# Transposing P by 64-row pairs, x a group ahead, and q scaled on ScalarE, in a cached-attention kernel

## The chip, the cores and the metric

The kernel runs on one core of one Trainium2 chip. The metric is the device time of one execution in microseconds. Executions of one kernel mostly agree within some 0.3% (an execution over 1.5% above its kernel's fastest would be called slow and left out). Ratios are the mean time of one kernel's fast runs over that of the other's fast runs of the same rounds, so they are not quite the ratio of the medians quoted beside them. "Faster" or "slower" needs 2%.

PSUM is the memory that TensorE writes its results to; it is divided into banks, and emptying a bank is called eviction here. A *row tile* is a group of rows of TensorE's array that works as a smaller array of its own.

Two more words are used throughout. A *step* is one group of four heads of one pair of batches: 128 steps make the run. A *phase* is 32 steps with one set of weights: there are four, and between them comes a *weight switch*.

## The reference, cut to what matters

Two independent attention blocks (A and B), each with 16 batches, 64 queries, 32 heads of 128, and a cache of 512 keys:

```python
q = (x @ wq).reshape(B, Sq, H, Dh).transpose(0, 2, 1, 3)          # x: 16 x 64 x 640
scores = einsum("bhqd,bhkd->bhqk", q, k_cache) * (Dh ** -0.5)     # k_cache: 16 x 32 x 512 x 128, bf16
p = softmax(scores)
o = einsum("bhqk,bhkd->bhqd", p, v_cache)
out = o.transpose(0, 2, 1, 3).reshape(B, Sq, H * Dh) @ wo         # wo: 4096 x 640
```

Nearly all bytes are K and V: each is read once. One step reads two K tiles and two V tiles of 512 KB.

## The kernel before: the parts that matter

A planner gives each operation a place in time, `AT`, in units of a step; the place sets only the order on each engine and the order in which SyncE queues the loads. Waits follow from what each operation reads and writes. Rings give the depth: six steps of K (`NK = 6`), four of V (`NV = 4`).

```python
AT = dict(XT=-0.998, XE=-0.828, XS=1.064, QP=-0.639, QE=-0.339, KT=(-1.008, -0.378), S=0,
          EX=(0.14, 0.192, 0.454, 0.611), RC=(0.31, 0.63), NM=(0.476, 0.739, 0.793, 0.91), TR=(0.854, 1.001),
          TE=(0.983, 1.034), PV=1.464, OE=1.653, OP=2.236, OA=2.301, OV=2.96, ST=3.466, ...)
# QP: Q projection (TensorE)        QE: scale q out of PSUM       KT: K transposed by VectorE
# S: scores (TensorE)               EX: exp (ScalarE)             NM: P times 1/sum (GpSimd)
# TR: transpose P (TensorE)         TE: copy P^T out of PSUM      PV: P @ V (TensorE)
# OE: O out of PSUM (ScalarE)       OP: output projection         XT: transpose x (TensorE)
```

The three operations that the change touches:

```python
def em_TR(e, op):                          # two per step: 8 transposes of 128 x 128 into one PSUM bank
    for t in range(8):
        last = e.transpose(pt_ps[:, t, :], pn_ring[:, op.idx % NPN, t].rearrange("q s k -> q (s k)"), ident[:, :])

def em_QE(e, op):                          # on VectorE
    ins = e.tensor_scalar(qs_ring[:, op.idx % NQ]..., ps[:, 0, :], scale, None, ALU.mult)

def em_PV(e, op):                          # 64 matmuls; s = 0 and 1 are row halves of the array, in two banks
    for a in range(2):
        for b in range(2):
            for t in range(8):
                for s in range(2):
                    rows = slice(64 * s, 64 * s + 64)
                    last = e.matmul(o_ps[:, s, col:col + 64], v_ring[rows, n % NV, b, a, t, :],
                                    pT_ring[rows, (2 * n + a) % NT, t, 64 * b:64 * b + 64],
                                    start=(t == 0), stop=(t == 7), tile_position=(64 * s, 0))
```

## Time and profile before

| what | before |
|---|---|
| time, median of 3 runs | 779.46 us (779.11 to 781.23) |
| span of the profiled run | 777.3 us |
| bytes moved, mean rate | 295.20 MB, 380 GB/s |
| TensorE, VectorE, ScalarE, GpSimd busy | 91%, 78%, 53%, 51% |

From the page of the kernel before: the row of the DMA engines' rate in 40 slices of the span, and the groups of the P transposes (matmuls, then weight loads), of P @ V and of the scaling of q. In a group line the numbers after the first bar are the busy time in us and the mean of one instruction in ns.

```profile
GB/s 318 389 395 397 394 396 395 394 396 391 392 387 399 398 400 400 400 394 394 387 389 395 397 397 397 397 397 398 374 387 388 398 398 399 400 398 400 400 254 15
...
L632 PE MATMUL ps<-ident,pn_ring 128*128 128x128 bf16 x2048 | 159.8, 221 | 2.7 <-DVE pT_ring L638 1.3
L632 PEld LDWEIGHTS ps<-ident,pn_ring 128*128 128x128 bf16 x2048 | 115.7, 98 | 65.8 <-DVE pT_ring L638 51.2
L650 PE MATMUL ps<-pT_ring,v_ring 64*128 64x64 bf16 x8192 | 142.3, 190 | 7.7 <-DMA v_ring<-in_A_v_cache_dram 4.0
...
L573 DVE TENSOR_SCALAR qs_ring<-ps 128x512 bf16<-128x512 f32 x128 | 85.3, 667 | 0.6 <-PE ps L567 0.5
```

I take some 400 GB/s for all that these engines give here; and TensorE is 91% busy at the same time: the kernel has two limits close to one another, and neither figure says which one counts where.

The window table of the same run, for the steady stretch of the fourth phase, and for two stretches around the end of the loads. The columns are: the window, its length, busy us (and instructions) of TensorE's matmuls, its weight loads, VectorE, ScalarE and GpSimd, then the granted clock, the mean share of the DMA engines, and GB/s.

```profile
620.00:736.00 116.00, 114.84 (x2957) 87.32 (x2977) 99.68 (x175) 68.51 (x197) 56.51 (x84) 1.00 1.04 399
746.00:750.00 4.00, 3.08 (x55) 1.82 (x41) 2.49 (x4) 1.85 (x7) 0.23 (x1) 1.00 0.98 348
750.00:754.00 4.00, 3.98 (x123) 2.71 (x121) 4.00 (x8) 1.20 (x4) 2.69 (x4) 1.00 0.20 75
```

In 620-736 us the DMA engines move 399 GB/s and TensorE is busy for 114.84 of 116 us. By 750 us the rate has collapsed: the loads are over but for stragglers, and 27 us of computing remain.

A step's rhythm, from TensorE's timeline (start in us, duration in us, line, operation; the output projection's lines are left out). P @ V is L650, the P transposes L632, scores L590, the Q projection L567.

```profile
703.53 1.28 PE L567 MATMUL ps<-xT_ring,wqp_sb 128*128 128x128 bf16 x20
704.74 1.11 PE L650 MATMUL ps<-pT_ring,v_ring 64*128 64x64 bf16 x64
705.78 0.62 PE L632 MATMUL ps<-ident,pn_ring 128*128 128x128 bf16 x8
706.33 1.13 PE L590 MATMUL ps<-kt_ring,qs_ring 32*64 32x512 bf16 x32
707.40 0.62 PE L632 MATMUL ps<-ident,pn_ring 128*128 128x128 bf16 x8
...
708.94 1.28 PE L567 MATMUL ps<-xT_ring,wqp_sb 128*128 128x128 bf16 x20
710.16 1.02 PE L650 MATMUL ps<-pT_ring,v_ring 64*128 64x64 bf16 x58
```

From one P @ V to the next there are 5.42 us (704.74 to 710.16). Over the run the intervals repeat as 5.41, 5.42, 5.41, 5.69 us; the fourth holds the transposes of x.

### The profile page before, as it was taken

To read this page: it belongs to the slowest core of one execution; us is meant where nothing else is said; L and a number is where in the kernel's file an instruction comes from. 1 tells how busy PE (TensorE), PEld (TensorE's weight loads), DVE (VectorE), ACT (ScalarE), POOL (GpSimd) and SP (SyncE) were. 2 spreads that over 40 slices of the span, in tenths; PEclk is the share of its full clock that TensorE was granted. 3 is DMA by queue.
4 is the path that set the end of the run, shared out by engine and by line. 5 is a ranking of instruction groups with operands and counts; after the bars stand their busy time and mean duration, and the time that the engine had idled before them with its cause. 6 is when DMAs were issued, how large, how long until landed. Compare 5 with 4: busy or idle time off the path is not lost.

```text
span 777.3 us, 40034 instructions
## 1 busy us (share of the span) xinstructions
PE 708.3 (91%) x17953; PEld 534.6 (69%) x18081; DVE 607.9 (78%) x1062; ACT 412.2 (53%) x1185; POOL 394.6 (51%) x566
## 2 busy tenths in 40 slices
PE   4559999999999999999988999999987899999994
PEld 3446777777777777777765777777765677777763
DVE  3537888888888888888766888888866788888873
ACT  2235656555555555555544555556554456565642
POOL 5424455555944454544843455454773454545441
PEclk9979999999999999999998999999999999999999
DMA  8999999999999999999999999999999999999960
GB/s 318 389 395 397 394 396 395 394 396 391 392 387 399 398 400 400 400 394 394 387 389 395 397 397 397 397 397 398 374 387 388 398 398 399 400 398 400 400 254 15
DMA packets 130096, 295.20 MB, mean 380 GB/s; under 512 B 9216, under 2 KB 31744, under 8 KB 130048
## 3 DMA queue, kind: packets, MB, share of 16 engines
q1 hardware_dynamic: 127744, 292.06, 99.4%
q10 hardware_dynamic: 2304, 2.62, 0.9%
q8 instruction: 15, 0.25, 0.1%
q14 instruction: 33, 0.27, 0.1%
HBM read 292.03 MB, written 2.62 MB: 379 GB/s over the span
## 4 chain that ended last, share of the span: by engine, by line
PE 54%; SPq 27%; DMA 14%; issue 2%; DVE 2%; ACT 0%; DVEq 0%; ACTq 0%
SPq L531 13%; PE ps L567 11%; PE ps L590 11%; SPq L524 11%; PE ps L632 11%; PE ps L650 11%; PE ps L666 7%; DMA kn_ring<-in_B_k_cache_dram 6%; DMA v_ring<-in_A_v_cache_dram 5%; PE ps L669 4%; DMA kn_ring<-in_A_k_cache_dram 2%; SPq L517 2%; DMA xn_ring<-in_A_x_dram 1%; DVE kt_ring L580 1%; PE ps L545 1%
## 5 line engine op out<-in xcount | busy, mean ns | idle before, releaser
L625 POOL TENSOR_SCALAR pn_ring<-p_ring,recip 128x512 bf16<-128x512 bf16 x512 | 344.9, 692 | 360.8 <-DVE recip L620 360.5
L605 ACT ACTIVATE p_ring<-ps 128x512 bf16<-128x512 f32 x512 | 298.7, 596 | 163.8 <-PE ps L590 161.2
L580 DVE STREAM_TRANSPOSE kt_ring<-kn_ring 128x1024 f32<-128x1024 f32 x256 | 315.1, 1231 | 41.1 <-DMA kn_ring<-in_B_k_cache_dram 24.6
L638 DVE COPY pT_ring<-ps 128x1024 bf16<-128x1024 bf16 x256 | 172.1, 672 | 56.9 <-PE ps L632 56.4
L657 ACT ACTIVATE oT_ring<-ps 128x512 bf16<-128x512 f32 x128 | 76.4, 597 | 183.3 <-PE ps L650 163.4
L590 PE MATMUL ps<-kt_ring,qs_ring 32*64 32x512 bf16 x4096 | 147.8, 397 | 24.6 <-DVE qs_ring L573 23.7
L567 PE MATMUL ps<-xT_ring,wqp_sb 128*128 128x128 bf16 x2560 | 166.8, 221 | 2.4 <-POOL wqp_sb L539 1.2
L567 PEld LDWEIGHTS ps<-xT_ring,wqp_sb 128*128 128x128 bf16 x2560 | 153.0, 114 | 18.8 <-ACT p_ring L605 2.2
L632 PE MATMUL ps<-ident,pn_ring 128*128 128x128 bf16 x2048 | 159.8, 221 | 2.7 <-DVE pT_ring L638 1.3
L632 PEld LDWEIGHTS ps<-ident,pn_ring 128*128 128x128 bf16 x2048 | 115.7, 98 | 65.8 <-DVE pT_ring L638 51.2
L650 PE MATMUL ps<-pT_ring,v_ring 64*128 64x64 bf16 x8192 | 142.3, 190 | 7.7 <-DMA v_ring<-in_A_v_cache_dram 4.0
L650 PEld LDWEIGHTS ps<-pT_ring,v_ring 64*128 64x128 bf16 x8192 | 126.9, 95 | 20.8 <-DMA v_ring<-in_A_v_cache_dram 5.4
L669 PE MATMUL ps<-wo_sb,oT_ring 128*128 128x128 bf16 x512 | 112.9, 220 | 8.0 <-ACT oT_ring L657 0.9
L666 PE MATMUL ps<-wo_sb,oT_ring 128*128 128x512 bf16 x384 | 119.6, 383 | 0.0
L605 ACT ACTIVATION_READ_ACCUMULATOR p_ring<-ps 128x1 f32 x512 | 105.1, 205 | 0.0
L590 PEld LDWEIGHTS ps<-kt_ring,qs_ring 32*64 32x64 bf16 x4096 | 55.4, 104 | 66.2 <-DVE qs_ring L573 26.6
L573 DVE TENSOR_SCALAR qs_ring<-ps 128x512 bf16<-128x512 f32 x128 | 85.3, 667 | 0.6 <-PE ps L567 0.5
L666 PEld LDWEIGHTS ps<-wo_sb,oT_ring 128*128 128x128 bf16 x512 | 50.5, 99 | 47.1 <-issue 1.7
L679 DVE TENSOR_TENSOR acc<-acc,ps 128x128 f32<-128x128 f32 x96 | 27.5, 287 | 49.0 <-PE ps L669 48.6
L669 PEld LDWEIGHTS ps<-wo_sb,oT_ring 128*128 128x128 bf16 x512 | 50.5, 99 | 0.0
L620 DVE RECIPROCAL recip<-rowsum 128x2 f32<-128x2 f32 x256 | 36.1, 141 | 2.9 <-ACT p_ring L605 2.8
L545 PE MATMUL ps<-ident,xn_ring 128*128 128x128 bf16 x160 | 15.0, 227 | 16.5 <-ACT oT_ring L657 10.4
(25 smaller groups left out, 121.1 us busy)
## 6 DMA issues: line engine op xcount, KB each, us to landing
kn_ring<-in_A_k_cache_dram SPq DMA_DIRECT2D x128, 512.0 KB, 12.4
v_ring<-in_A_v_cache_dram SPq DMA_DIRECT2D x128, 512.0 KB, 11.6
kn_ring<-in_B_k_cache_dram SPq DMA_DIRECT2D x128, 512.0 KB, 12.5
v_ring<-in_B_v_cache_dram SPq DMA_DIRECT2D x128, 512.0 KB, 10.2
ws_ring<-in_A_wq_dram SPq DMA_DIRECT2D x8, 640.0 KB, 12.2
wo_sb<-in_A_wo_dram SPq DMA_DIRECT2D x8, 640.0 KB, 12.3
ws_ring<-in_B_wq_dram SPq DMA_DIRECT2D x8, 640.0 KB, 12.5
wo_sb<-in_B_wo_dram SPq DMA_DIRECT2D x8, 640.0 KB, 12.6
```

What stands on the lines that cost most here:

```text
L524: ins = e.dma_start(kn_ring[:, n % NK, b, :], src)
L531: ins = e.dma_start(v_ring[:, n % NV, b].rearrange("p a t d -> p a (t d)"), src)
L567: last = e.matmul(ps[:, 0, f * 128:(f + 1) * 128], w[:, kt, f, :], xT_ring[:, xs, kt, :], start=(kt == 0), stop=(kt == KT - 1))
L580: ins = e.transpose(dst, kn_ring[:, n % NK, b, :].bitcast(F32))
L590: last = e.matmul(ps[64 * b:64 * b + 64, i, :], qs_ring[rows, n % NQ, f, b, :], kt_ring[rows, n % NKT, b, :, f // 2, :, f % 2], start=(f = ...
L605: ins = e.activation(dst, src, ACTF.Exp, scale=1.0, accum_out=rowsum[:, h:h + 1])
L625: ins = e.tensor_scalar(pn_ring[:, (h // 2) % NPN, :, h % 2, :], p_ring[:, (h // 2) % NP, :, h % 2, :], recip[:, (h // 2) % NR, h % 2:h % ...
L632: last = e.transpose(pt_ps[:, t, :], pn_ring[:, op.idx % NPN, t].rearrange("q s k -> q (s k)"), ident[:, :])
L638: ins = e.tensor_copy(pT_ring[:, op.idx % NT].rearrange("p t q -> p (t q)"), pt_flat)
L650: last = e.matmul(o_ps[:, s, col:col + 64], v_ring[rows, n % NV, b, a, t, :], pT_ring[rows, (2 * n + a) % NT, t, 64 * b:64 * b + 64], star ...
L666: last = e.matmul(out_ps0, oT, wo_sb[:, 4 * j + h4, 0:N0], start=(j == 0 and h4 == 0), stop=(j == NJ - 1 and h4 == 3))
L669: last = e.matmul(out_ps1, oT, wo_sb[:, 4 * j + h4, N0:D], start=(h4 == 0), stop=(h4 == 3))
```

## The change

Its intent: give TensorE and VectorE less to do.

- P is transposed by 16 matmuls of 64 rows instead of 8 of 128, alternating between the row halves of the array, as P @ V does. The Trainium skill (TensorEngine Tiling (Array Packing), Key Properties and Gotcha 1) says that row tiles load weights and multiply in parallel, but must not write one PSUM bank at the same time; hence the two banks. The second one is shared with O, so transposes, their copies, P @ V and the eviction of O now exclude one another (`B5`).
- x is transposed in the bank of the output projection, between two groups, one group ahead, kept in SBUF, and copied by GpSimd.
- q is scaled by ScalarE instead of VectorE.
- All places `AT` were set anew, so the orders of the engines and of the loads differ too.

```diff
-    AT = dict(XT=-0.998, XE=-0.828, XS=1.064, QP=-0.639, QE=-0.339, KT=(-1.008, -0.378), S=0,
-              EX=(0.14, 0.192, 0.454, 0.611), RC=(0.31, 0.63), NM=(0.476, 0.739, 0.793, 0.91), TR=(0.854, 1.001),
-              TE=(0.983, 1.034), PV=1.464, OE=1.653, OP=2.236, OA=2.301, OV=2.96, ST=3.466, WP0=-1.75, WP1=-2.974)
+    AT = dict(XT=-2.594, XE=-2.103, XC=-0.826, QP=-0.625, QE=-0.284, KT=(-1.051, -0.379), S=0,
+              EX=(0.262, 0.298, 0.389, 0.649), RC=(0.547, 0.697), NM=(0.571, 0.642, 0.8, 1.158), TR=(1.059, 1.236),
+              TE=(1.121, 1.538), PV=1.655, OE=1.933, OP=2.167, OA=2.291, OV=2.255, ST=3.374, WP0=-1.75, WP1=-1.488)
 ... (x: load queued earlier, XT into the output bank, XE into xs_sb, XC copies xs_sb to xT_ring; cut)
-        add("dve", "QE", n, n + AT["QE"], [], [("SB", 0), ("qs", n % cfg.NQ)])
+        add("act", "QE", n, n + AT["QE"], [], [("SB", 0), ("qs", n % cfg.NQ)])
 ...
-                [("PTB",)])
-            add("dve", "TE", m, n + AT["TE"][a], [], [("PTB",), ("pT", m % cfg.NT)])
+                [("B5",)])
+            add("dve", "TE", m, n + AT["TE"][a], [], [("B5",), ("pT", m % cfg.NT)])
 ... (PV and OE likewise from OB to B5; waits that move with it; cut)
-        OUT_BANK, O_BANK, PT_BANK = 4, 5, 7
-        pt_flat = ps[:, PT_BANK, :].bitcast(BF16)
-        pt_ps = pt_flat.rearrange("p (t q) -> p t q", t=8)
+        PT_BANK, O_BANK, OUT_BANK = 4, 5, 7
+        pt_flat = ps[:, PT_BANK:PT_BANK + 2, :].bitcast(BF16)[:, :, 0:512]
 ...
-            ins = e.tensor_scalar(qs_ring[:, op.idx % NQ].rearrange("p f b q -> p (f b q)"), ps[:, 0, :], scale, None,
-                                  ALU.mult)
+            ins = e.activation(qs_ring[:, op.idx % NQ].rearrange("p f b q -> p (f b q)"), ps[:, 0, :], ACTF.Copy,
+                               scale=scale)
 ...
             for t in range(8):
-                last = e.transpose(pt_ps[:, t, :], pn_ring[:, op.idx % NPN, t].rearrange("q s k -> q (s k)"),
-                                   ident[:, :])
-                first = first or last
+                for b in range(2):
+                    rows = slice(64 * b, 64 * b + 64)
+                    last = e.transpose(pt_flat[:, b, 64 * t:64 * t + 64],
+                                       pn_ring[rows, op.idx % NPN, t].rearrange("q s k -> q (s k)"),
+                                       ident[rows, rows], tile_position=(64 * b, 0))
+                    first = first or last
```

The new order on TensorE is: P @ V, scores, first P transpose, output projection, second P transpose, Q projection. Before it was: P @ V, first P transpose, scores, second P transpose, output projection, Q projection.

## The prediction

> **What bounds the kernel now.** Two things, one after the other. The page gives 295.2 MB moved, and the slices show the DMA engines full from start to almost the end (window table: share 1.04; 399 GB/s in 620-736 us, 380-390 GB/s where weights are loaded with K and V). The last bytes land near 751 us; the span ends at 777.3 us, so about 26.5 us of computing are left when the loads are over. Between the weight switches TensorE sets the pace: it is 97-99% busy in 60-190, 230-340, 420-540 and 620-736 us, and P@V starts come every 5.41, 5.42, 5.41, 5.69 us (mean 5.48), which the timeline shows to be filled with matmuls. K and V of one step are 2.097 MB, at 399 GB/s 5.25 us. So in the last phase the loads run ahead of the arithmetic until the rings stop them (the queue waits 48.8 us for P@V to free V buffers), and this lead is the long tail. In the first 50 us TensorE also waits some 14 us for the second x tile (wait list: eviction of O <- x load, 14.9 us), but the DMA moves 389-396 GB/s meanwhile.
>
> **What the change does, per step of 128.**
> - TensorE: two transposes of 8 x 128 rows (0.45 us each) become 16 x 64-row ones, alternating between row halves. P@V has that very form: 64 in 0.99 us, so 16 need about 0.25 us: saving 0.4 us. The Trainium skill (TensorEngine Tiling (Array Packing), Key Properties) says that row tiles run in parallel, which P@V agrees with, and that changing the tiling mode drains the array. There are two more mode changes per step; from P transposes before scores (0.55 us against 0.45 us of loads) I estimate 0.1 us each. Net 0.2 to 0.4 us: a step of 5.1 to 5.25 us.
> - VectorE loses the scaling of q (0.67 us), ScalarE gains about 0.6 us. ScalarE is 53% busy, VectorE 78%: good.
> - x goes through a saved copy, 0.7 us on GpSimd once in four steps, off the path. The earlier x load should end the 14 us stall, without saving DMA time.
> - The second transpose bank is now shared with O. Transpose, copy, transpose, copy, P@V, eviction are serial: 0.25+0.7+0.25+0.7+1.1+0.6 us plus handoffs, about 4.3 us, under 5.2 us, with other matmuls between.
>
> **Critical path.** Loads cannot end much earlier: a little is won where the queue waits for buffers (397 against 399 GB/s; 363-387 GB/s in 548-568 us). I expect 746-750 us. With computing at the loads' pace the tail is only the latency after the last loads: from the start of the last P@V to the end took 10.1 us (767.2 to 777.3, 6 us of it the store); the last K needs transpose, scores, exp, normalisation, transposes first, so 12 to 16 us. Span about 761 us; measured time is 2.2 us longer.
>
> **Prediction: 763 us, 2.1% faster, 8 in 10 within 755 to 771.** Faster by over 2%: 0.53; within 2%: 0.45; slower by over 2%: 0.02.
>
> **What would show it.** P-transpose groups of about 0.25 us; P@V intervals of 5.1-5.3 us, DMA-paced, with more idle TensorE and waits for K or V landings; queue waits for P@V much below 48.8 us; DMA still at 395-400 GB/s; time from last landing to end 12-16 us instead of 26.5; no 14 us wait near 35-50 us.
>
> **What would make it wrong.** If the shared bank stalls TensorE or mode changes eat the saving, steps stay at 5.4 us and the time is 770-779 us. If the last K is issued further ahead, or loads gain more from freer buffers, 755 us.

## More of the kernel before

TensorE's program is long, so its middle is a hardware loop of four steps:

```python
lo = next(i for i, o in enumerate(pe) if o.kind == "QP" and o.idx == cfg.FIRST)               # FIRST = 4
hi = next(i for i, o in enumerate(pe) if o.kind == "QP" and o.idx == cfg.FIRST + cfg.PERIOD)  # PERIOD = 4
reps = (N - 1 - cfg.FIRST) // cfg.PERIOD                                                      # 30 turns
...
for op in prog[:lo]:                       # straight code
    emit(e, op, p, {})
with e.Fori(0, reps):                      # the loop: steps 4 to 123
    ...
for op in prog[lo + size * reps:]:         # straight code again: the end of the run
    emit(e, op, p, taken)
```

## The result, and the profile after

The kernel after takes 778.58 us (median of 4 runs, 777.16 to 779.55) against 779.91 us before in the same rounds: ratio 0.998, 95% interval 0.9958 to 1.0002. The time is the same. The forecast of 763 us, and its range of 755 to 771 us, were wrong.

The lines of the page after that answer to those of before:

```profile
GB/s 313 388 395 397 396 393 397 393 396 393 389 388 399 399 398 401 399 394 398 387 387 393 397 397 397 396 398 398 386 378 389 395 398 400 399 400 399 400 258 16
...
L656 PE MATMUL ps<-pT_ring,v_ring 64*128 64x64 bf16 x8192 | 142.7, 191 | 24.2 <-DMA v_ring<-in_B_v_cache_dram 11.1
...
L637 PEld LDWEIGHTS ps<-ident,pn_ring 64*128 64x128 bf16 x4096 | 74.6, 95 | 108.6 <-ACT oT_ring L663 58.9
...
L637 PE MATMUL ps<-ident,pn_ring 64*128 64x64 bf16 x4096 | 105.1, 192 | 17.2 <-DVE pT_ring L644 11.2
...
L576 ACT ACTIVATE qs_ring<-ps 128x512 bf16<-128x512 f32 x128 | 76.4, 597 | 23.4 <-PE ps L570 23.4
```

TensorE's matmuls are busy 34 us less (708.3 to 674.1 us), VectorE 64 us less. Q's scaling takes 597 ns on ScalarE instead of 667 on VectorE. The rates of the DMA engines are nearly those of before, slice by slice. So the work went away, and the time did not.

The windows after, for the same stretches:

```profile
620.00:736.00 116.00, 110.05 (x3362) 81.38 (x3380) 91.64 (x157) 79.20 (x215) 61.97 (x93) 1.00 1.04 399
746.00:750.00 4.00, 2.65 (x29) 1.50 (x30) 0.69 (x1) 1.26 (x4) 0.00 (x0) 0.61 0.96 354
750.00:754.00 4.00, 3.83 (x126) 2.89 (x132) 3.45 (x7) 2.43 (x6) 1.80 (x3) 0.96 0.26 95
```

TensorE has 5 us more idle time in 620-736 us. In 746-750 us it is busy for only 2.65 of 4 us, and its granted clock, which is 1.00 before the change, is down to 0.61 there.

The rhythm of a step after (P @ V is L656, scores L593, transposes L637, Q projection L570):

```profile
702.69 1.11 PE L656 MATMUL ps<-pT_ring,v_ring 64*128 64x64 bf16 x64
703.76 1.14 PE L593 MATMUL ps<-kt_ring,qs_ring 32*64 32x512 bf16 x32
704.83 0.41 PE L637 MATMUL ps<-ident,pn_ring 64*128 64x64 bf16 x16
...
706.36 0.41 PE L637 MATMUL ps<-ident,pn_ring 64*128 64x64 bf16 x16
706.70 1.31 PE L570 MATMUL ps<-xT_ring,wqp_sb 128*128 128x128 bf16 x20
707.95 1.11 PE L656 MATMUL ps<-pT_ring,v_ring 64*128 64x64 bf16 x64
```

Here a step takes 5.26 us (702.69 to 707.95). Over the run the intervals repeat as 5.22, 5.50, 5.25, 5.65 us: a mean of 5.405 against 5.4825 us before. I had forecast 5.1 to 5.25.

And the end of the run. These are TensorE's instructions after idle time for which the trace shows no releaser ("issue": the sequencer had nothing to hand on), from the timeline, first of the kernel before in 740-748 us, then of the kernel after in 739-749 us. The bracket gives the idle us before the instruction.

```profile
741.73 0.23 PE L632 MATMUL ps<-ident,pn_ring 128*128 128x128 bf16 x1 [0.73 <-issue]
...
747.66 0.43 PE L590 MATMUL ps<-kt_ring,qs_ring 32*64 32x512 bf16 x6 [0.86 <-issue]
```

```profile
740.60 0.23 PE L675 MATMUL ps<-wo_sb,oT_ring 128*128 128x128 bf16 x1 [1.87 <-issue]
...
747.01 0.65 PE L593 MATMUL ps<-kt_ring,qs_ring 32*64 32x512 bf16 x7 [2.54 <-issue]
...
748.54 0.31 PE L675 MATMUL ps<-wo_sb,oT_ring 128*128 128x128 bf16 x1 [0.34 <-issue]
```

All of these fall behind the loop, where TensorE has passed into straight code: its timeline puts the Q projection of step 124, the first operation behind the loop, at 736.57 us before and at 733.87 us after. The second stall after has a sequel: in the window 748-750 us the granted clock is 0.50, and from the first P transpose there to the second it takes 2.79 us (747.59 to 750.38), against 1.53 us at full clock. A ledger of the span makes the account. It is worked out from the starts of P @ V in the timelines; steps are counted from 0, step 100 is the first one clear of the last weight switch, step 127 the last.

| | start of P@V 100 | 22 steps, 100 to 122 | five steps, 122 to 127 | from there to the end | span |
|---|---|---|---|---|---|
| before | 617.0 | 120.8 (5.49 a step) | 29.4 | 10.1 | 777.3 |
| after | 615.7 | 119.4 (5.43 a step) | 32.0 | 10.1 | 777.2 |

The change gains 1.3 us up to step 100, 1.4 us in the next 22 steps, and gives 2.6 us back in the five steps behind the loop.

### The profile page after: what moved, and what is told of

The parts are those of the page before. It is cut to its first block, busy times and chain, and to the rows that moved or that the text cites. A ratio compares the mean times of both kernels' runs of the same rounds, so it can differ in the third digit from the quotient of the medians.

```text
span 777.2 us, 44414 instructions
## 1 busy us (share of the span) xinstructions
PE 674.1 (87%) x20001; PEld 492.0 (63%) x20129; DVE 544.4 (70%) x934; ACT 484.3 (62%) x1297; POOL 404.8 (52%) x582
## 4 chain that ended last, share of the span: by engine, by line
PE 41%; SPq 25%; DMA 18%; POOL 5%; issue 5%; DVE 4%; ACT 0%; DVEq 0%; ACTq 0%
SPq L528 12%; SPq L535 11%; PE ps L570 9%; PE ps L656 9%; PE ps L593 8%; DMA v_ring<-in_B_v_cache_dram 7%; PE ps L672 6%; POOL pn_ring L628 5%; PE ps L637 5%; DMA v_ring<-in_A_v_cache_dram 5%; PE ps L675 4%; DMA wo_sb<-in_B_wo_dram 2%; DMA kn_ring<-in_B_k_cache_dram 2%; DMA wo_sb<-in_A_wo_dram 2%; DVE pT_ring L644 2%
## 5 line engine op out<-in xcount | busy, mean ns | idle before, releaser
L583 DVE STREAM_TRANSPOSE kt_ring<-kn_ring 128x1024 f32<-128x1024 f32 x256 | 312.8, 1229 | 79.9 <-DMA kn_ring<-in_B_k_cache_dram 47.7
L644 DVE COPY pT_ring<-ps 128x1024 bf16<-128x1024 bf16 x256 | 176.2, 688 | 78.8 <-PE ps L637 72.6
L570 PE MATMUL ps<-xT_ring,wqp_sb 128*128 128x128 bf16 x2560 | 170.6, 223 | 19.8 <-issue 13.6
L570 PEld LDWEIGHTS ps<-xT_ring,wqp_sb 128*128 128x128 bf16 x2560 | 151.0, 115 | 28.8 <-issue 16.4
L656 PE MATMUL ps<-pT_ring,v_ring 64*128 64x64 bf16 x8192 | 142.7, 191 | 24.2 <-DMA v_ring<-in_B_v_cache_dram 11.1
L593 PE MATMUL ps<-kt_ring,qs_ring 32*64 32x512 bf16 x4096 | 148.0, 398 | 8.5 <-issue 6.1
L656 PEld LDWEIGHTS ps<-pT_ring,v_ring 64*128 64x128 bf16 x8192 | 127.3, 95 | 38.9 <-DMA v_ring<-in_B_v_cache_dram 14.5
L637 PEld LDWEIGHTS ps<-ident,pn_ring 64*128 64x128 bf16 x4096 | 74.6, 95 | 108.6 <-ACT oT_ring L663 58.9
L637 PE MATMUL ps<-ident,pn_ring 64*128 64x64 bf16 x4096 | 105.1, 192 | 17.2 <-DVE pT_ring L644 11.2
L672 PE MATMUL ps<-wo_sb,oT_ring 128*128 128x512 bf16 x384 | 119.4, 382 | 0.0
L608 ACT ACTIVATION_READ_ACCUMULATOR p_ring<-ps 128x1 f32 x512 | 101.7, 199 | 0.0
L576 ACT ACTIVATE qs_ring<-ps 128x512 bf16<-128x512 f32 x128 | 76.4, 597 | 23.4 <-PE ps L570 23.4
L593 PEld LDWEIGHTS ps<-kt_ring,qs_ring 32*64 32x64 bf16 x4096 | 56.0, 104 | 42.7 <-issue 8.0
L685 DVE TENSOR_TENSOR acc<-acc,ps 128x128 f32<-128x128 f32 x96 | 27.4, 285 | 37.4 <-PE ps L675 37.2
L542 POOL COPY wqp_sb<-ws_ring 128x1280 bf16<-128x1280 bf16 x16 | 20.0, 1253 | 15.6 <-DMA ws_ring<-in_A_wq_dram 8.2
```

The costliest lines, as they stand in the source:

```text
L570: last = e.matmul(ps[:, 0, f * 128:(f + 1) * 128], w[:, kt, f, :], xT_ring[:, xs, kt, :], start=(kt == 0), stop=(kt == KT - 1))
L583: ins = e.transpose(dst, kn_ring[:, n % NK, b, :].bitcast(F32))
L593: last = e.matmul(ps[64 * b:64 * b + 64, i, :], qs_ring[rows, n % NQ, f, b, :], kt_ring[rows, n % NKT, b, :, f // 2, :, f % 2], start=(f = ...
L608: ins = e.activation(dst, src, ACTF.Exp, scale=1.0, accum_out=rowsum[:, h:h + 1])
L637: last = e.transpose(pt_flat[:, b, 64 * t:64 * t + 64], pn_ring[rows, op.idx % NPN, t].rearrange("q s k -> q (s k)"), ident[rows, rows], t ...
L644: ins = e.tensor_copy(pT_ring[:, op.idx % NT].rearrange("p b t q -> p b (t q)"), pt_flat)
```

## The experiments

The theories put to the test, as they arose:

- **A**: up to the last weight switch TensorE waits for loads in any case, so only what comes behind it counts: the pace of some 22 steps, and the stalls that TensorE suffers as it leaves its loop for straight code while the DMA engines are full.
- **B** (rival): the loads alone set the time, with a fixed latency behind them, whatever TensorE does.
- **C**: without the stalls, the end is the landing of the last K plus the pipeline's depth, so K should be loaded earlier.

All numbers of the ledger kind come from one profiled execution of each kernel; times are medians over the rounds. In each round the kernel before ran on the same chip: 780.11 us in the first two calls, 779.91 and 779.47 us in the third and fourth.

### Leaving the loop later

```diff
-    FIRST = 4
+    FIRST = 6        # a_exit6: the loop covers steps 6 to 125 instead of 4 to 123
```

> The kernel after, with TensorE's loop starting two steps later, so that it is left two steps later (step 125 instead of 123); nothing else changes. Theory A (leaving the loop while the loads still fill the DMA engines costs TensorE two instruction-fetch stalls of 1.9 and 2.5 us near 740-747 us): the exit falls at about 749 us, when the loads end, the stalls shrink below 1 us each, and the end comes 3 to 4 us earlier, ratio to before about 0.993 to 0.995. Rival B (the loads alone set the time, whatever TensorE does, with a fixed latency behind them): 778 us as after, within 1 us.

Measured: 773.16 us, ratio to before 0.9912 (0.9895 to 0.9928). The last five steps take 26.0 us instead of 32.0, the 22 steps before them 119.1 instead of 119.4 us. In 733-765 us no stall of the kind shown above is over 0.24 us. Theory A under-estimated the gain: 5.4 us were won, not 3 to 4. It also had the exit later than it is: the loop is left at 744.7 us, not 749, with the loads still at 388 GB/s until 748 us. Why the stalls vanish all the same is shown below, with the blocks of instructions. Theory B falls.

### Less work per step

```diff
-                for kt in range(KT):
+                for kt in range(KT - 1):      # a_qp4: one k-tile of five left out; wrong result
```

> The kernel after, wrong on purpose: the Q projection contracts over four of five k-tiles, which takes some 0.23 us from TensorE's step and changes no wait and no load. Theory A: the mean step becomes about 5.17 us, below the 5.25 us the loads need, so in the last stretch TensorE catches up with the loads by 4 to 5 us and waits for them; stalls at the loop exit remain: about 772 to 774 us. Rival B (step time does not matter, loads and a fixed latency do): 778 us. My prediction's simple form (below 5.25 us the whole tail of 26 us falls to 12-16): about 765 us.

Measured: 776.83 us, ratio 0.996 (0.9943 to 0.9976). The 22 steps take 118.8 us (5.40 a step), only 0.6 us less than after, though TensorE has some 0.2 us less to do in each: TensorE waits for loads instead. Within 616-735 us P @ V's weight loads wait for V of block B 18 times, 6.0 us in all, against twice and 0.7 us in the kernel after. From the wait list of the whole run, for block B (engine, line, what it waited for, us in total, times, longest); K's transposes are L583, P @ V L656. In the kernel after the second of these is 14.5 us, 19 times:

```profile
DVE kt_ring L583 <- DMA kn_ring<-in_B_k_cache_dram: 53.7, 51, 4.1
...
PEld ps L656 <- DMA v_ring<-in_B_v_cache_dram: 26.6, 47, 2.4
```

My prediction in its simple form (765 us) falls with this run, and Theory A's 772 to 774 us is missed as well: the step cannot get below 5.40 us, and the reason is arithmetic I had done wrongly. Four steps of the last phase load 16 tiles of 512 KB (8.389 MB) and also store one output tile of 160 KB (0.164 MB), which I had left out: 8.553 MB at the 399 GB/s of the windows are 21.4 us, 5.36 us a step instead of 5.25. The room below the 120.8 us of before was therefore 2.0 us in all, and the change took 1.4 of them.

### The edge of the loop moved

```diff
-    FIRST = 4
+    FIRST = 2
-    lo = next(i for i, o in enumerate(pe) if o.kind == "QP" and o.idx == cfg.FIRST)
+    lo = next(i for i, o in enumerate(pe) if o.kind == "TR" and o.idx == 2 * cfg.FIRST + 1)   # hi likewise
-    reps = (N - 1 - cfg.FIRST) // cfg.PERIOD
+    reps = (N - 1 - cfg.FIRST) // cfg.PERIOD - 1
```

> The kernel after, with the loop's edge put before the second P transpose (behind the output projection's long matmuls) instead of before the Q projection (behind the short transposes); the exit stays at the same step within 0.2 steps. Theory A: one step in four loses its bubble of about 0.4 us at the loop's jump: P@V intervals 5.22, 5.50, 5.25, 5.25 instead of 5.22, 5.50, 5.25, 5.65 us; over the 22 steps after the last weight switch this is 2 us. Time about 776.5 us. If the 5.65 us step has another cause than the jump, it stays.

Measured: 778.15 us, ratio 0.9982 (0.9965 to 0.9998). The fourth interval falls from 5.65 to about 5.4 us (5.37, 5.39, 5.40, 5.37 in the last phase, and one of 5.62), not to the 5.25 expected, so part of it was the jump behind short matmuls. But the 22 steps end at the same 118.8 us as the run before: the loads' pace. And 30.9 us are spent in the last five steps: the stall of the exit is still there, with the loop's edge elsewhere in the code. The ratio to before is that of the kernel after (0.998); the 776.5 us expected are missed.

### Both

```diff
     FIRST = 4        # a_both: the edge at the second P transpose as above, and 30 turns from there
```

> The kernel after with the loop's edge before the second P transpose and, with it, the exit 1.9 steps later. Theory A: both gains add: steps mean 5.3 us and no exit stall under load: 771 to 774 us, ratio 0.990 to 0.993. Rival B: 778 us.

Measured: 773.65 us, ratio 0.9926 (0.9903 to 0.9949). The ledger reads 615.9, 118.8, 26.7 and 10.5 us. This is a_exit6 again, not better: with the exit stall all but gone (0.90 us are left), TensorE's pace is worth no more than the 0.3 us that 118.8 is below 119.1.

### The kernel before, with a later exit

```diff
-    FIRST = 4
+    FIRST = 7        # b_exit7, on the kernel before
```

> The kernel before, with its loop starting three steps later, so left three steps later (step 126). Theory A: its exit stalls were 0.7 and 0.9 us while loads ran; gain 1 to 2 us, about 778 us: less than the same shift gives the kernel after. Rival B: no change.

Measured: 781.12 us, ratio 1.0001 (0.9979 to 1.0024): no change, but not for the rival's reason. The last five steps shrink from 29.4 to 26.8 us, as Theory A has it. Step 100, however, starts at 621.8 instead of 617.0 us. The rate line of its page shows where that comes from:

```profile
GB/s 318 389 396 396 320 362 398 392 397 394 392 386 396 398 401 398 401 394 398 384 392 392 397 398 396 397 397 396 389 387 390 391 400 399 399 400 399 398 306 16
```

In the fifth and sixth slices the rate falls to 320 and 362 GB/s, where before it was 394 and 396. The intervals of P @ V in the loop's first turn are 7.97, 7.42 and 11.33 us. TensorE is late there, the rings are full, and the queue waits for P @ V (104.6 us in the queue's own wait list, against 48.8 before). The loads lose bandwidth at the start that nothing gives back. The trace shows what held TensorE up: blocks of 16 KB of its instructions arrive at 74.78, 81.21 and 88.73 us, and each time its weight loads, idle for 1.35, 2.16 and 3.31 us, go on 1.3 to 1.5 us later. Such waits for instructions are taken up again below. Why this kernel has more of them here than before has is not shown.

### The transposes undone

```diff
-                for b in range(2):
-                    ...pairs of 64 rows into two banks
+                last = e.transpose(pt_ps[:, t, :], pn_ring[:, op.idx % NPN, t]..., ident[:, :])   # a_tr128
```

> The kernel after with one part undone: each P transpose is again 8 matmuls of 128 rows into one bank; order, waits and everything else stay as after. Theory A: the pair form saves only about 0.1 us a transpose net of the mode changes, so the step grows from 5.40 to about 5.5-5.6 us, and in the last stretch (22-27 steps) 3 to 5 us are lost, partly given back by a shorter exit stall (half as many instructions): about 779 to 782 us. If the pair form saved 0.2 us each as predicted, the base step would be 5.62 us and the time 784 us or more.

Measured: 775.26 us, ratio 0.9935 (0.9919 to 0.9952): *faster* than the whole change by some 3 us, where I had expected it equal or slower. The ledger reads 616.0, 120.4 (5.47 a step), 26.7 and 10.2 us. So the pair form saves 1.0 us over 22 steps, 0.05 us a step, and the old form has no exit stall. The same stretch of a step in this kernel (transposes L636, output projection from the first L670 on, Q projection L571, P @ V L654):

```profile
705.88 0.62 PE L636 MATMUL ps<-ident,pn_ring 128*128 128x128 bf16 x8
706.34 0.38 PE L670 MATMUL ps<-wo_sb,oT_ring 128*128 128x512 bf16 x1
...
707.43 0.61 PE L636 MATMUL ps<-ident,pn_ring 128*128 128x128 bf16 x8
707.87 1.28 PE L571 MATMUL ps<-xT_ring,wqp_sb 128*128 128x128 bf16 x20
709.09 0.58 PE L654 MATMUL ps<-pT_ring,v_ring 64*128 64x64 bf16 x28
```

From the first transpose to the second it takes 1.55 us (705.88 to 707.43), against 1.53 us (704.83 to 706.36) with pairs; from the second to the Q projection 0.44 against 0.34 us; from there to P @ V 1.22 against 1.25 us. The pairs' own loads of weights take 0.29 us instead of 0.45 in the timelines, so of a gross 0.16 us each, 0.02 and 0.10 us are left, less 0.03. Where the first transpose stands between scores (row tiles of 32) and the output projection (128), nothing is won: with pairs TensorE's timeline has 0.16 us of idle time before the output projection, with the old form none. The Trainium skill (TensorEngine Tiling (Array Packing), Key Properties) says that a change of tiling mode drains the array, and gives no figure. The idle time may be such a drain; no run isolates it.

### q back on VectorE

```diff
-        add("act", "QE", n, n + AT["QE"], ...)      # and em_QE as before
+        add("dve", "QE", n, n + AT["QE"], ...)      # a_qdve
```

> The kernel after with q scaled by VectorE again (0.67 us), order kept. If ScalarE's taking it over is what keeps VectorE off the path: steps lengthen by up to 0.3 us, about 783 us. If TensorE sets the pace with room on both: unchanged within 1 us of after.

Measured: 783.49 us, ratio 1.0044 (1.0027 to 1.0061). The 22 steps take 126.8 us, 5.76 a step, and scores wait for q on VectorE. In the new order this part of the change is needed: it is worth 7.4 us of the last stretch. The last five steps take 27.4 us here, and the exit stall is absent, though TensorE's code is as long as in the kernel after and its loop is left at the same step. That comes later, at 742.3 us, and in 744-746 us the DMA engines are down to 158 GB/s.

### The x load alone

```diff
-            loads.append((txt - 0.1, ...))
+            loads.append((txt - 2.4, ...))          # b_xearly, on the kernel before
```

> The kernel before with the load of x queued 2.3 steps earlier, nothing else. Theory A: the 14 us wait of TensorE near 35-50 us goes, and the time does not change (779 us within 1 us), because the lag it leaves is absorbed at the first weight switch, where TensorE waits for loads anyway.

Measured: 780.27 us, ratio 0.9999 (0.9982 to 1.0016), step 100 at 617.5 us. But the wait did not go. The planner puts the x load behind the moment when the single x buffer comes free, so its issue moved only from 34.80 to 34.43 us, and the long interval of P @ V is 20.3 us instead of 19.7. The run misses its aim. The kernel after answers the question better: there no interval of the first steps is above 11 us, and step 100 still starts only 1.3 us earlier.

### K ahead of V

```diff
-            loads.append((tk - 0.05, ready, 2, op))
+            loads.append((tk - 1.05, ready, 2, op))     # a_e6_k1 and b_k1; tk - 2.05 in a_e6_k2
```

> The kernel after with the later loop exit, and each K load queued one step earlier than the V loads it had stood behind. Theory C (with the exit stall gone the end is the landing of the last K plus the depth of the pipeline: 747.5 us + 13.8 us to the last P@V + 10.4 us): the last K lands about 2.6 us earlier, and the end comes 2 to 3 us earlier than in a_exit6, about 770.5 us. Rival A2 (TensorE's pace still sets the end): 773 us as a_exit6.

> The same with K two steps earlier. Theory C: another 2 us or so at most, until the last V (755.8 us + 10.4 us) bounds the end: 768 to 770 us. If V then comes too late for P@V in the middle of the run: back to 773 us.

> The kernel before with each K load queued one step earlier. Theory C applied to before: last K landed at 750.6 us and 26.7 us remained, of which 2.2 us were exit stalls; TensorE's own pace (5.48 us against 5.35 us) is the slower one here, so little is gained: 778 to 780 us. If the order of loads alone explained what the kernel after gains beside its exit stall: about 776 us.

Measured: 776.57 us (0.9953, 0.9936 to 0.9969), 780.71 us (1.0026, 1.0004 to 1.0047), and on the kernel before 779.88 us (0.9999, 0.9982 to 1.0016). Theory C falls. Step 100 starts at 619.9 and 622.8 us, against 616.2 in a_exit6. Of this delay 2.0 and 2.7 us are there by step 8, and the rest comes at the first two weight switches (3.7 and 6.8 us in all by step 64). I read it as V losing what K gains; the wait lists do not show it clearly. From step 100 the 22 steps take 119.5 and 119.2 us, so the delay is carried to the end. The last five steps, at 25.6 us, are hardly below a_exit6's 26.0. So the last K's landing is not what ends these runs; the position at step 100 counts for more. The landing times quoted in these expectations came from the records of single transfers in the trace.

### Later exit and less work

> The kernel after with the later loop exit and, wrong on purpose, one k-tile less in the Q projection (0.2 us less TensorE work a step). Theory C: the loads pace the last stretch already (K, V and stores of four steps are 8.55 MB, 21.4 us at 399 GB/s, 5.35 us a step), so a faster step gains nothing beyond a_exit6 except in the steps after the last K: 772 to 773 us. Rival A2 (TensorE's step still matters with a weight of 22 steps): 768 to 770 us.

This kernel joins the edits of a_exit6 and a_qp4. Its output is wrong, which doesn't matter for the time. Measured: 772.66 us, ratio 0.9908 (0.9891 to 0.9924): 616.0, 118.8, 25.4 and 10.5 us. This number is as Theory C had it, but C has fallen; what it shows is the loads' pace in the 22 steps once more, and Rival A2 (768 to 770 us) falls. A TensorE that does 0.2 us less in each of 128 steps wins at most half a microsecond, which is within the noise. From the last K transpose on VectorE to the end it takes 20 us even here. That transpose in the timelines of before, after and a_exit6:

```profile
755.87 1.22 DVE L580 STREAM_TRANSPOSE kt_ring<-kn_ring 128x1024 f32<-128x1024 f32 x1
```

```profile
757.03 1.23 DVE L583 STREAM_TRANSPOSE kt_ring<-kn_ring 128x1024 f32<-128x1024 f32 x1
```

```profile
750.81 1.23 DVE L583 STREAM_TRANSPOSE kt_ring<-kn_ring 128x1024 f32<-128x1024 f32 x1
```

With the spans of 777.3, 777.2 and 771.7 us, 21.4, 20.2 and 20.9 us are left from its start; in a_e6_qp4, where it starts at 750.44 of 770.8 us, 20.4 us. So this length is the same with the exit stall and without: the stall lies in front of this transpose. Nor does the transpose start when its K lands. In a_exit6 the last K lands at 748.0 us, 2.8 us before; in the kernel after at 747.5 us, 9.5 us before; and none of the three lines shows idle time of VectorE in front of it: in VectorE's program it stands behind the work of earlier steps. The chain behind it (scores, exp, normalisation, transposes, P @ V and output projection, spread over more than two steps of the program's order, and a store) has a length that the change hardly touches. I had put 12 to 16 us.

### What makes the exit stall

One cause was open: why the stall came with the pair transposes and not with the old ones, at the same exit. The page's list of DMA queues has two that carry instructions. The packets of one of them go with the number of TensorE's instructions: 15 in both kernels with the old transposes, 17 with pairs, 16 in a_qp4. Its line (packets, MB, share of the engines' time) in the kernel after and in a_tr128:

```profile
q8 instruction: 17, 0.28, 0.2%
```

```profile
q8 instruction: 15, 0.25, 0.1%
```

The 17 packets of 0.28 MB are 16 KB each. The Trainium skill (Runtime: NRT & Kernel Launch, Instruction fetch mechanics) says that each engine's instructions come in blocks of 16 KiB over the sequencer's own DMA queue, that crossing a block's border is mostly hidden, and that a taken branch breaks the sequential prefetch. The packets' size agrees. If this is the cause, it must matter where the borders fall. Two kernels shift TensorE's code by repeating the very first x transposes, long before the loop:

```diff
-            for kt in range(KT):
+            for kt in list(range(KT)) * (6 if op.idx == 0 else 1):     # a_pad6; 13 in a_pad13
```

> The kernel after, loop exit unmoved, with the very first x transposes issued six times over before the loop (25 more matmuls and their weight loads, about a fifth of a 16 KB page of instructions), which only shifts where TensorE's code lies. If the exit stalls come from where the page borders fall: the last five steps change by over 1 us from 32.0 us, either way. If they come from leaving the loop under load, wherever the borders fall: 31 to 32 us again, 778 us.

> The same with thirteen repetitions (60 more matmuls and weight loads, about half a page). Page borders: the last five steps differ from those of after and of the six-fold one; at some shift they should fall towards the 26 to 27 us of the runs without a stall. Load alone: 31 to 32 us in all three.

Measured: 775.20 us (2 runs, ratio 0.9944, 0.9926 to 0.9962) and 779.10 us (2 runs, 0.9994, 0.9973 to 1.0015). The last five steps take 28.0 and 27.9 us, against 32.0 in the kernel after. The longest stalls that are left behind the loop, two in a_pad6 and one in a_pad13, from their timelines:

```profile
742.91 1.14 PE L593 MATMUL ps<-kt_ring,qs_ring 32*64 32x512 bf16 x32 [0.97 <-DVE kt_ring L583]
...
749.29 0.61 PE L656 MATMUL ps<-pT_ring,v_ring 64*128 64x64 bf16 x29 [1.28 <-issue]
```

```profile
751.05 1.11 PE L656 MATMUL ps<-pT_ring,v_ring 64*128 64x64 bf16 x64 [1.68 <-DVE kt_ring L583]
```

The trace puts two of these down to a K transpose. But P @ V does not read K, and before both, TensorE's weight loads are marked "issue".

So 25 matmuls more, far away and harmless, take 4 us off the end. The other half of the last expectation, that thirteen repetitions give a third value, did not come true: 28.0 and 27.9 us are the same.

The traces hold the proof as well: the time of each packet of this queue. In the kernel after no block arrives between 70.3 and 738.0 us, while TensorE goes round its loop. The first two blocks behind the loop, and TensorE's stalls there (end of the packet, then the start of the next matmul, in us):

| | first block | TensorE goes on | idle | second block | TensorE goes on | idle |
|---|---|---|---|---|---|---|
| before | 740.43 | 741.73 | 0.73 | 746.40 | 747.66 | 0.86 |
| after | 739.16 | 740.60 | 1.87 | 745.72 | 747.01 | 2.54 |
| a_anchor2 | 738.66 | 739.97 | 1.91 | 745.07 | 746.39 | 1.09 |
| a_qp4 | 739.36 | 740.83 | 0.81 | 745.74 | 747.11 | 2.39 |
| a_pad6 | 741.50 | 742.91 | 0.97 | 748.02 | 749.29 | 1.28 |
| a_pad13 | 743.27 | 744.52 | 0.78 | 749.65 | 751.05 | 1.68 |

Each stall ends 1.25 to 1.47 us after a block has arrived, and from the end of the first stall to the end of the second the trace holds 255 or 256 instructions of TensorE in each of these runs, the same number each time, as blocks of one size would give. (b_xearly and b_k1, on the kernel before, show the same.) So TensorE stands at the borders of its blocks and waits for the next one, and that is shown. How long it stands depends on what lies in a block: in the kernel after the first one is used up in 3.87 us, in a_pad6 and a_pad13 in 5.10 and 4.86, in the kernel before in 5.06 us, while the next arrives 5.9 to 6.6 us after the one before it. And it depends on the load: once the loads are over, blocks arrive as little as 3.4 us apart, and in a_qdve, with the code of the kernel after but the DMA engines down to 158 GB/s behind its loop, there is no stall. In a_exit6 the first block behind the loop comes at 749.6 us, when the loads end. The old transposes alone do not avoid the stall: a_tr128 has none, the kernel before has two.

a_pad13 gains as much at the end and loses it earlier (step 100 starts at 618.3 us); why it is late there is open, and with two runs a kernel its time is a rough one. What decides when a block is asked for is open as well.

### The best version, and whether the pairs are worth anything

```diff
-    FIRST = 4
+    FIRST = 6        # a_exit6_r5: the kernel after; a_tr128_e6: the same with the old transposes
```

> The kernel after with the later loop exit again, byte for byte, with five rounds, as the version that beats both: 773 us, ratio 0.990 to 0.992.

> The kernel after with the later loop exit and the P transposes in their old form of 8 x 128 rows. If the pair form is worth anything once its exit stall is out of the way: 773.5 to 774.5 us, about 1 us above a_exit6 (steps 5.47 us against 5.41 us over 22 steps). If it is worth nothing: equal to a_exit6 within 0.5 us.

Measured in five rounds side by side: 773.45 us (0.9918, 0.9904 to 0.9931) and 773.46 us (0.9922, 0.9909 to 0.9936). The kernel after with its loop left two steps later beats both kernels, the one before by 0.8% and the one after, by way of the ratios to before, by 0.6%; both are clear of noise though under 2%. With the old transposes it is just as fast. The pair form, the headline of the change, is worth nothing measurable in the time.

The ledger of the runs that the argument rests on:

| | P@V 100 | 22 steps | last five steps | to the end | span | time, ratio |
|---|---|---|---|---|---|---|
| before | 617.0 | 120.8 | 29.4 | 10.1 | 777.3 | |
| after | 615.7 | 119.4 | 32.0 | 10.1 | 777.2 | 778.58, 0.998 |
| a_tr128 | 616.0 | 120.4 | 26.7 | 10.2 | 773.3 | 775.26, 0.9935 |
| a_qp4 | 615.8 | 118.8 | 29.8 | 10.1 | 774.4 | 776.83, 0.996 |
| a_exit6 | 616.2 | 119.1 | 26.0 | 10.4 | 771.7 | 773.16, 0.9912 |
| a_e6_qp4 | 616.0 | 118.8 | 25.4 | 10.5 | 770.8 | 772.66, 0.9908 |
| a_e6_k2 | 622.8 | 119.2 | 25.6 | 10.2 | 777.8 | 780.71, 1.0026 |
| a_qdve | 616.8 | 126.8 | 27.4 | 10.3 | 781.2 | 783.49, 1.0044 |

## Why the prediction was wrong, point by point

**Right.** The bytes, their rate (395 to 400 GB/s where only K and V come) and so the end of the bulk of the loads near 750 us did not move. TensorE's busy time fell as costed (34 us, of 26 to 51), VectorE's by 64 us of the 85 that the scaling of q had taken, ScalarE takes 0.6 us for q, and the shared bank stalls nothing that counts: from scores to the next transpose it is 1.07 us in both kernels (706.33 to 707.40, and 703.76 to 704.83). Ending the long stall over the second x tile saved no time worth naming. P @ V's waits for V did rise, and the queue's waits for P @ V fell from 48.8 to 15.6 us.

**Wrong, the step that failed**: "With computing at the loads' pace the tail is only the latency after the last loads: ... 12 to 16 us. Span about 761 us." Its premise failed first: steps of 5.1 to 5.25 us, at the loads' pace or below, did not come (5.405 us on the mean). That is the case that the prediction names under what would make it wrong, with 770 to 779 us. But the sum would have failed with the premise met: a_qp4 and a_e6_qp4, made faster on purpose, take 776.83 and 772.66 us. Three terms of it were off.

1. *The lead that was to vanish was small.* I read 26.5 us of computing after the loads as a lead that the loads had gained over a slow TensorE. TensorE goes at the loads' pace through each weight switch (some 7.1 us a step), so a lead can grow only behind the last one, over 22 steps, and there the loads' own pace is 5.36 us, not 5.25, because the output stores were left out of the sum. The floor, measured by taking work away (a_qp4, a_e6_qp4; a_anchor2 and a_both reach it too), is 118.8 us against 120.8 before. So a faster step could win 2.0 us there, not the ten or more of the forecast.
2. *The latency behind the loads was mis-sized.* From the last K transpose on, 20.2 to 21.4 us remain in the four runs above, not 12 to 16; and the transpose does not follow its K's landing at once (2.8 us in a_exit6, 9.5 us in the kernel after). It is the depth of the program's order, not a latency behind the last load: moving K ahead did not shorten the run. In a_exit6, without the stall, 750.8 us and 20.9 us make the span of 771.7 us, which is 10.7 us above the 761 of the forecast.
3. *A cost was missing.* Leaving the loop cost the kernel after 6.0 us in the last five steps (32.0 against 26.0 in a_exit6), 3.4 us more than it cost before (29.4 against 26.8 in b_exit7). Of the 6.0 us, 4.4 are the two waits for instruction blocks and some 1.3 the slow stretch at half the clock behind the second. The change made TensorE's code longer and moved the borders of its blocks while the DMA engines were full. Without this cost the kernel gains 0.9% (a_exit6), with it 0.2%; a_tr128 and a_exit6 are both faster than the whole change.

**The size of the pair form** was off too: I had 0.2 to 0.4 us a step net, the runs show 0.05 us of mean step (119.4 against 120.4 us over 22 steps), with some 0.10 us in a plain step and part of that lost in the fourth step of each turn (5.65 against 5.59 us), which has the loop's jump. That changes of the tiling mode at the edges of the transposes eat the rest is my reading, not shown.

**What would have shown it beforehand**: the intervals of P @ V around the weight switches (7 to 8 us each, all load-paced) say that time won earlier is lost there; the packets of the instruction queue could be timed; and the two exit stalls of 0.73 and 0.86 us were already in the trace of before.

What stays open: what triggers the fetch of a block; why b_exit7 has more such waits early in the run, and why a_pad13 is late there; where the pair form's saving goes; and the floor of about 616 us at step 100, which I put down to loads, though no experiment here took any away.

## What to carry to other kernels

Where a kernel is load-paced at regular points, count a faster engine only from the last such point to the end, and work out the loads' pace with every byte in it, stores too. Measure the room first by taking work away on purpose: two wrong-result runs showed here that a faster step could win 2 us, not 16. And look at where a hardware loop is left: here the straight code behind it stalled for up to 4.4 us in all, waiting for its instructions while the DMA engines were full, and moving the exit by two steps was worth more than the whole change.

## What the Trainium skill lacked or had wrong

- Runtime: NRT & Kernel Launch, Instruction fetch mechanics, calls the cost of crossing a 16 KiB border mostly hidden. Behind a loop, with the DMA engines at 403 and 388 GB/s, TensorE stood still for 1.87 and 2.54 us until a block came; with the code shifted by 25 matmuls the last five steps went from 32.0 to 28.0 us, and with the exit two steps later, so that the first block came as the loads ended, to 26.0 us. The section gives no time for a block: under full load they came 5.9 to 6.6 us apart in the six runs of the table, and TensorE went on 1.25 to 1.47 us after each.
- TensorEngine Tiling (Array Packing), Key Properties, says that a change of tiling mode drains the array, but gives no figure. No run here isolates one either: of 0.16 us that a transpose by pairs saves in weight loading, 0.02 us were left between scores and output projection, and 0.10 us, less 0.03 in what follows, between output projection and Q projection.
- HBM Reference gives about 425 GB/s for a core that streams alone. With 512 KB transfers of K and V this core moved 399 GB/s at a DMA share of 1.04, and 374 to 390 where weights were loaded too; the record does not say what the other core of the pair did.
